# Loading the keys' weights ahead of the tokens in a one-core attention-and-MLP kernel

## The chip, the core and the metric

The kernel runs on one core of a Trainium2 chip. A core has five engines that run side by side, each through its own list of instructions: TensorE (PE, matrix products; its weight loads are shown as PEld), VectorE (DVE), ScalarE (ACT), GpSimd (POOL) and SyncE (SP). In this kernel SP only issues DMA transfers. An engine takes its instructions strictly in order and waits at one until its inputs are there. The metric is device time in microseconds (us) of one execution, as the median of several runs.

## The reference

The input `x` has 2048 tokens of 512 features, in bf16. It is normalised once (`xn`, a layer norm without gain), and two branches read it; their sum is added to `x`.

```python
def _A_ref(x, wqkv, w_phi, wo):        # 32 heads of 16
    q, k, v = split(x @ wqkv)
    pq = einsum("bhsd,hdf->bhsf", q, w_phi)
    pk = einsum("bhsd,hdf->bhsf", k, w_phi)
    phi_q = concat([softmax(pq), softmax(-pq)])     # over the 16 features of a head
    phi_k = concat([softmax(pk), softmax(-pk)])
    kv  = einsum("bhsf,bhsd->bhfd", phi_k, v)
    z   = einsum("bhsf->bhf", phi_k)
    num = einsum("bhqf,bhfd->bhqd", phi_q, kv)
    den = einsum("bhqf,bhf->bhq", phi_q, z)[..., None] + 1e-6
    return (num / den) @ wo

def _B_ref(x, w1, b1, w2):             # 1792 hidden units
    h = x @ w1 + b1
    return (h * tanh(softplus(h))) @ w2

xn = layernorm(x)
out = x + _A_ref(xn, wqkv, w_phi, wo) + _B_ref(xn, w1, b1, w2)
```

## The kernel before

**Tiles.** The 2048 tokens are 16 tiles of 128, in four groups of four. All of `x` stays in `x_sb`; the normalised and transposed tokens stay in `xnT`, in which the features lie on the partitions.

**Folded weights.** The product of a head's `wqkv` columns with its `w_phi` does not depend on the tokens. So the kernel computes the folded keys' weights first (`wkp`, 512 x 512) and projects tokens with them directly. `Wbd` is a block-diagonal arrangement of `w_phi` (tile `wsrc`). Folding needs the keys' weights transposed (`wT`): the row blocks 2 and 3 of the weights come transposed by a DMA (line 483), and the row blocks 0 and 1 come as they are into `wkp` (line 482) and are transposed by TensorE against an identity, then copied into `wT`.

**Order of the work.** Nothing reorders instructions: `manual_schedule` is set, and the string `STEPS` (line 24) is an order written out by a planning run. The loop at line 648 calls one small function per step, and each function appends its instructions to the engines' lists. The `@` number of a step is the PSUM bank, one of six, that it writes; a letter at the end says which engine does a copy or a root (`a` ScalarE, `v` VectorE, `p` GpSimd). So the order of steps is the order in which each engine meets its own instructions. The loads at the start stand ahead of `STEPS` (lines 477 to 493), and the transfers issued by SP start in the order in which SP issues them.

**The head.** These steps come first, until TensorE can run on without pauses:

| step | what it does | engine | line |
|---|---|---|---|
| warm-up | matmuls on constants (`WARM` of 512 columns, `SHORT` of 128) | PE | 514 |
| `LS i`, `RS i` | mean and variance of token tile i; reciprocal root | DVE; ACT or POOL | 165 and 167; 557 or 171 |
| `AZ i` | normalise tile i | DVE | 176 |
| `TP i`, `TC i` | transpose tile i on TensorE; copy it into `xnT` | PE; DVE or ACT | 569; 588 |
| `TW kt`, `TK kt` | transpose row block kt of the keys' weights; copy into `wT` | PE; ACT | 576; 582 |
| `WB` | build `Wbd` from `wsrc` | DVE | 528 |
| `F0 kt`, `FD kt` | fold row block kt; copy it into `wkp` | PE; ACT or DVE | 151; 160 |
| `LP` | keys' logits of token tiles 0 and 1, eight matmuls, row block by row block | PE | 204 |
| `V t`, `VC t` | values of tile t; copy out | PE; ACT or DVE | 189; 213 |
| `L s i`, `LC s i` | logits of tile i of group s; copy out (groups 0 to 3 are keys, 4 to 7 queries) | PE; ACT or DVE | 189; 247 |
| `PB`, `CB` | transpose the bias `b1`; copy it out | PE; DVE | 537; 629 |
| `AM` | load the activation table for the hidden layer | ACT | 139 |

`LP` is ordered by row block: its first two matmuls need `xnT` of tiles 0 and 1 and row block 0 of the folded weights, its last two need row block 3. `FD kt` writes over `wkp`, in which row blocks 0 and 1 lay as they came.

**The rest.** For each group: statistics and normalisation (`LN`, `AP`; `AP` also issues a transposing DMA into `xnT`), the hidden layer (`H` on PE, `M` on ACT, 56 of each), the softmax features (`E` on DVE, `X` on ACT, sums `S` on DVE, `R` and `N` or `W`), the keys' sums into PSUM (`A`, a matmul of features with values, which needs `N`), the masked sums (`KV`), then for queries `Q`, `G`, `C`, and for each token tile the second layer and output projection into one bank (`O`, `P`), the residual and the store (`Y`). The last tile is split in two parts (`OH`, `PH`, `YH`). `DX` and `DW` load further tokens and weights, and `WT` loads and transposes the queries' weights, whose fold is `F`, `FC`.

Of the kernel before, what the change touches and what calls it, by code (L numbers as in the profile page):

```python
# [27 lines left out]
H 10 @0; M 8; H 11 @2; H 12 @1; LN 1; M 9; E 0 0; AP 1 0; AP 1 1; H 13 @4; L 1 0 @3; DX 3; L 1 3 @5;  # L30
DW 2; E 0 1; X 0 1; LN 2; LC 1 0 v; LC 1 3 v; WL 1; LN 3; AP 2 0; AP 2 1; X 0 0; V 6 @3; M 10; M 11;
M 12; H 14 @5; S 0 0; WL 2; LC 1 2 a; VC 6 a; M 13; AP 3 0; H 15 @0; H 16 @2; H 17 @1; LC 1 1 a; AP
3 1; WT; H 18 @3; H 19 @4; M 14; M 15; M 16; M 17; H 20 @5; M 18; M 19; H 21 @0; H 22 @2; H 23 @1; H
24 @3; M 20; M 21; H 25 @4; H 26 @5; M 22; M 23; H 27 @0; M 24; M 25; M 26; M 27; H 28 @2; M 28; H
29 @1; M 29; E 1 0; E 1 1; S 0 1; L 2 1 @3; L 2 0 @4; LC 2 0 v; L 2 2 @5; LC 2 1 v; L 2 3 @0; F 0
@2; R 0 0 a; L 3 2 @1; R 0 1 a; LC 2 2 v; LC 2 3 a; FC 0 a; X 1 0; F 1 @4; F 2 @3; FC 2 a; N 0 0; L
3 0 @5; V 9 @0; LC 3 0 a; V 3 @2; VC 3 a; LC 3 2 v; A 0 0; VC 9 a; V 7 @1; F 3 @3; V 2 @5; VC 7 a; V
8 @2; L 3 3 @0; FC 3 a; X 1 1; VC 2 a; FC 1 v; E 2 0; L 4 0 @4; DW 3; LC 3 3 a; E 2 1; V 4 @1; N 0
1; VC 8 v; X 2 0; S 1 1; LC 4 0 a; S 1 0; L 4 3 @3; VC 4 a; L 4 2 @5; V 11 @0; A 0 1; LC 4 2 a; V 5
@2; VC 11 a; R 1 1 a; S 2 0; L 4 1 @4; LC 4 1 a; L 3 1 @1; VC 5 a; LC 3 1 a; H 30 @5; H 31 @0; LC 4  # L40
3 v; R 1 0 a; M 30; H 32 @4; M 31; M 32; H 33 @2; M 33; N 1 1; H 34 @1; H 35 @3; H 36 @5; M 34; H 37
@0; M 35; H 38 @4; E 3 0; H 39 @2; H 40 @1; M 36; N 1 0; M 37; M 38; M 39; H 41 @3; H 42 @5; H 43
@0; M 40; A 1 0; M 41; E 3 1; M 42; M 43; A 1 1; X 2 1; V 12 @4; VC 12 a; L 5 0 @2; V 10 @1; V 15
@3; VC 15 a; V 13 @5; V 14 @0; E 4 0; E 4 1; LC 5 0 a; VC 13 v; VC 10 a; L 5 2 @4; X 3 1; X 3 0; L 6
3 @3; VC 14 a; L 5 3 @2; O 0 @5; LC 5 2 a; S 2 1; S 3 1; S 3 0; R 3 1 a; R 2 1 a; N 2 1; R 2 0 a; L
6 0 @1; R 3 0 a; N 3 0; L 5 1 @0; LC 5 1 a; N 3 1; O 1 @4; L 6 1 @0; LC 6 0 a; LC 6 3 a; L 6 2 @1; H
44 @3; X 4 0; N 2 0; S 4 0; LC 6 2 a; LC 6 1 v; LC 5 3 a; A 2 0; A 2 1; A 3 0; A 3 1; H 45 @1; X 4
1; M 44; W 4 0 v; H 46 @2; H 47 @0; M 45; M 46; S 4 1; M 47; KV; H 48 @3; M 48; H 49 @1; H 50 @2; M
49; H 51 @0; H 52 @3; M 50; M 51; Q 0 0; H 53 @1; G 0 0; H 54 @2; M 52; Q 0 1; H 55 @0; W 4 1 v; L 7
3 @3; M 53; M 54; E 5 0; G 0 1; L 7 0 @1; E 5 1; Q 1 0; C 0 a; O 2 @2; G 1 0; LC 7 0 a; X 5 0; Q 1  # L50
1; O 3 @1; G 1 1; E 6 0; S 5 0; P 0; P 1; C 1 a; LC 7 3 a; W 5 0 v; L 7 2 @3; M 55; Y 0; O 4 @0; O 5
@5; P 2; LC 7 2 a; Y 1; X 5 1; Q 2 0; G 2 0; L 7 1 @4; E 6 1; LC 7 1 a; P 3; S 5 1; Y 2; W 5 1 v; X
6 0; Q 2 1; G 2 1; O 6 @3; O 7 @2; E 7 0; C 2 a; S 6 0; Y 3; W 6 0 a; E 7 1; Q 3 0; O 8 @4; P 4; Y
4; G 3 0; X 6 1; Q 3 1; G 3 1; X 7 0; S 6 1; C 3 a; O 9 @1; P 5; X 7 1; W 6 1 v; Q 4 0; G 4 0; O 10
@0; Y 5; Q 4 1; G 4 1; S 7 0; C 4 a; O 11 @5; W 7 0 v; Q 5 0; G 5 0; P 6; P 7; Q 5 1; G 5 1; Y 6; O
12 @3; S 7 1; C 5 a; Q 6 0; W 7 1 a; P 8; P 9; G 6 0; Q 6 1; Y 7; Y 8; Y 9; G 6 1; O 13 @2; Q 7 0; C
6 v; G 7 0; P 10; P 11; Y 10; Q 7 1; O 14 @4; G 7 1; P 12; C 7 a; Y 11; Y 12; P 13; OH 0 @1; P 14;
PH 0; OH 1 @0; PH 1; Y 13; Y 14; YH 0; YH 1
"""


# [1 line left out]
def kernel(  # L63
# [410 lines left out]

    part = (slice(0, 384), slice(384, 512))

    for t in range(2):
        nc.sync.dma_start(x_sb[:, t, :], x_v[:, t, :])  # L478
# [3 lines left out]
    nc.sync.dma_start(wkp[:, 0:2, :], wqkv_v[:, 0:2, D : 2 * D])
    nc.sync.dma_start_transpose(
        out=wT_of[0][:, :, 2 * P : 4 * P], in_=A_wqkv[2 * P : 4 * P, D : 2 * D]
    )
    nc.scalar.dma_start(b1b[:], b1_v[:, :])
    with nc.allow_non_contiguous_dma(reason="tiny w_phi load"):
        nc.scalar.dma_start(wsrc[:], wphi_v)
    nc.sync.dma_start(x_sb[:, 2:4, :], x_v[:, 2:4, :])
# [23 lines left out]
    def dummy(n):  # L513
        nc.tensor.matmul(
            warm[:, 0:n], lhsT=nc.const_aps.tensor(1.0, [P, P], BF16),
            rhs=nc.const_aps.tensor(1.0, [P, n], BF16), start=True, stop=True,
        )
# [163 lines left out]
```

## Time and profile before

| | |
|---|---|
| median of 3 runs | 173.78 us (173.75 to 174.08) |
| the profiled execution, its own time | 173.71 us |
| its span | 172.0 us |
| TensorE busy | 168.0 us, 98% |
| VectorE busy | 143.9 us, 84% |
| ScalarE busy | 123.8 us, 72% |
| share of TensorE in the chain that ended last | 95% |

The span runs from the first to the last instruction of the trace; some 1.7 us of the execution lie around it. Times in the trace count from the start of the span. A row of the timeline gives the start, the length, the engine, the line, the operation with its output and input, how many of them were merged into the row, and, in brackets, how long the engine had been idle before it and what released it. SPq and ACTq are the issuing of DMA transfers on those engines. A view by stages gives for each stretch the busy time of each engine with its instruction count, the granted clock of TensorE, the share of the 16 DMA engines and what they moved.

### The profile page before, as it was taken

The page shows a single profiled execution, that of the slowest core. Times are in us where ns is not written, and L with a number is a line of the kernel's source. Part 1 is how long each engine was busy: PE and PEld are TensorE (multiplying, and loading weights), DVE is VectorE, ACT ScalarE, POOL GpSimd, SP SyncE. Part 2 cuts the span into 40 slices and gives each one's busy share as a digit, 9 for nine tenths or more (in the row PEclk, how much of TensorE's full clock was granted, in tenths as well). Part 3 has the DMA queues.
Part 4 walks back from the last instruction along what each step waited for, and adds up shares of the span by engine and source line. Part 5 has one row for each costly group of instructions (what it writes and reads, how often), then busy time and mean ns, then how long its engine had stood idle before and what let it go on. Part 6 is the DMA issues. An engine that isn't in the chain of part 4 may idle for free.

```text
span 172.0 us, 2735 instructions
## 1 busy us (share of the span) xinstructions
PE 168.0 (98%) x1047; PEld 82.6 (48%) x1047; DVE 143.9 (84%) x223; ACT 123.8 (72%) x199; POOL 7.8 (5%) x23
## 2 busy tenths in 40 slices
...
GB/s 124 303 370 248 54 255 347 99 162 228 21 0 0 0 4 0 0 0 0 4 0 0 36 113 99 61 9 150 90 97 116 153 52 197 146 134 216 110 131 61
DMA packets 44185, 18.02 MB, mean 105 GB/s; under 512 B 35980, under 2 KB 44172, under 8 KB 44172
## 3 DMA queue, kind: packets, MB, share of 16 engines
...
## 4 chain that ended last, share of the span: by engine, by line
PE 95%; DMA 2%; SPq 0%; ACT 0%; issue 0%; DVE 0%
PE po L457 28%; PE ph L223 28%; PE pl L189 14%; PE po L464 8%; PE pv L189 8%; PE pnd L412 2%; PE pkv L381 2%; DMA wkp<-in_A_wqkv_dram 2%; PE pl L204 1%; PE pfold L151 1%; PE pwide L189 1%; SPq L478 0%; PE ptr L569 0%; PE ptw L576 0%; ACT wT L582 0%
## 5 line engine op out<-in xcount | busy, mean ns | idle before, releaser
L457 PE MATMUL po<-w_sb,acts 128*128 128x512 bf16 (+2 forms) x238 | 50.8, 366 | 0.0
L223 PE MATMUL ph<-xnT,w_sb 128*128 128x512 bf16 x224 | 49.8, 379 | 0.0
L234 ACT ACTIVATE acts<-ph,b1f 128x512 bf16<-128x512 f32 x56 | 36.3, 701 | 4.2 <-PE ph L223 4.0
L300 DVE TENSOR_REDUCE s<-e 128x128 f32<-128x2048 bf16 x16 | 36.1, 2276 | 0.5 <-ACT e L283 0.5
L223 PEld LDWEIGHTS <-w_sb 128*128 128x128 bf16 x224 | 21.7, 98 | 25.7
L457 PEld LDWEIGHTS <-acts 128*128 128x128 bf16 x238 | 22.1, 98 | 23.6
L283 ACT ACTIVATE e<-e 128x2048 bf16<-128x2048 bf16 x16 | 30.5, 1919 | 0.0
L189 PEld LDWEIGHTS <-xnT 128*128 128x128 bf16 x184 | 17.5, 98 | 19.6
L471 DVE TENSOR_TENSOR x_sb<-po,x_sb 128x512 bf16<-128x512 f32 (+2 forms) x17 | 11.0, 656 | 8.4 <-PE po L464 8.4
L464 PE MATMUL po<-wqk,xnT 128*128 128x512 bf16 (+2 forms) x68 | 15.6, 366 | 0.0
L189 PE MATMUL pv<-wv,xnT 128*128 128x512 bf16 x64 | 15.6, 379 | 0.0
L189 PE MATMUL pl<-wqk,xnT 128*128 128x512 bf16 x64 | 15.4, 379 | 0.0
L427 ACT COPY ds<-pnd 128x32 f32<-128x32 f32 x16 | 2.9, 182 | 16.5 <-PE pnd L412 16.5
L247 ACT CAST p_sb<-pl 128x512 bf16<-128x512 f32 x21 | 12.2, 594 | 3.6 <-PE pl L189 3.4
L139 ACT ACT_TABLE_LOAD x10 | 12.8, 1283 | 0.2
L258 DVE TENSOR_TENSOR m<-m 128x512 bf16<-128x512 bf16 (+1 forms) x32 | 11.5, 359 | 1.1
L189 PE MATMUL pl<-wkp,xnT 128*128 128x512 bf16 x48 | 11.7, 379 | 0.0
L267 DVE TENSOR_TENSOR e<-p_sb,m 128x2048 bf16<-128x2048 bf16 x8 | 9.8, 1226 | 1.8 <-PE pkv L381 1.5
L258 DVE TENSOR_TENSOR m<-p_sb 128x1024 bf16<-128x1024 bf16 x16 | 10.9, 681 | 0.0
L165 DVE BATCH_NORM_STATS2 stats<-x_sb 128x6 f32<-128x512 bf16 x16 | 10.1, 677 | 0.9 <-DMA x_sb<-in_A_x_dram 0.9
L267 DVE TENSOR_TENSOR e<-m,p_sb 128x2048 bf16<-128x2048 bf16 x8 | 9.8, 1225 | 0.3
L334 DVE TENSOR_TENSOR e<-e,r 128x2048 bf16<-128x2048 bf16 x8 | 9.6, 1216 | 0.5 <-ACT r L309 0.5
...
## 6 DMA issues: line engine op xcount, KB each, us to landing
...
out_dram<-x_sb SPq DMA_DIRECT2D x15, 128.0 KB, 1.8
...
x_sb<-in_A_x_dram SPq DMA_DIRECT2D x2, 128.0 KB, 2.1
wkp<-in_A_wqkv_dram SPq DMA_DIRECT2D x1, 256.0 KB, 3.6
x_sb<-in_A_x_dram SPq DMA_DIRECT2D x1, 256.0 KB, 3.6
```

What stands on the lines that cost most here:

```text
L139: nc.scalar.preload_act_table_set(name)
L189: nc.tensor.matmul(pp, lhsT=xnT[:, t, kt, :], rhs=w[:, kt, :], start=(kt == 0), stop=(kt == KT - 1),)
L223: nc.tensor.matmul(ph_of[u][:], lhsT=w1_sb[:, kt, f * P : (f + 1) * P], rhs=xnT[:, g * TPG : (g + 1) * TPG, kt, :], start=(kt == 0), stop= ...
L234: nc.scalar.activation(acts[:, f, g * 512 : (g + 1) * 512], ph_of.pop(u)[:], ACT.Mish, bias=b1f[:, f : f + 1])
L247: copy(p_of[s][:, i, :], pl_of.pop((s, i)))
L258: nc.vector.tensor_tensor(out=m[:], in0=src[:, :, 0:half], in1=src[:, :, half : 2 * half], op=op)
L267: nc.vector.tensor_tensor(out=e_of[s][:].rearrange("p t j l c -> p (t j) l c")[:, :, pl, :].rearrange("p t (c e o) -> p t c e o", e=8, o=2 ...
L283: nc.scalar.activation(v, v, ACT.Exp)
L300: nc.vector.reduce_sum(t[:], pair(s, k).rearrange("p t j l (c e) -> p (t j l c) e", e=16), axis=AX.X)
L457: nc.tensor.matmul(po_of[t, c.stop][:, c], lhsT=acts[:, f, t * P : (t + 1) * P], rhs=w2_sb[:, f, c], start=(f == 0), stop=False,)
L464: nc.tensor.matmul(po_of[t, c.stop][:, c], lhsT=oT_of[t // 2][:, t % 2 * 4 + j, :], rhs=wo_sb[:, j, c], start=False, stop=(j == 3),)
L471: nc.vector.tensor_tensor(out=y, in0=po_of.pop((t, c.stop))[:, c], in1=y, op=ALU.add)
```

## The change

It touches the head in four ways, and the whole `STEPS` string was planned anew with it.

1. SP's loads are put in another order. Before: token tiles 0 and 1 (two transfers of 128 KB), the natural half of the keys' weights (256 KB), their transposed half, token tiles 2 and 3 (256 KB), then `wv`. After: the natural half of the keys' weights, token tiles 0, 1, 2 to 3, the transposed half, then `wv`. From `wv` on the order is the same.
2. On ACT's queue the load of `w_phi` comes first. The bias load, which was ahead of it, now stands behind the load of ScalarE's first activation table.
3. The warm-up matmuls ahead of the steps are six of 512 columns and three of 128, where nine and three stood. Three more of 512 columns (`AW`, which was a 128-column one that no step used) come behind `TW 1`.
4. The steps of the head are laid out anew. On TensorE: `TW 0`, `TW 1`, three `AW`, `F0 0`, `F0 1`, `TP 0`, `TP 1`, `PB`, `F0 2`, `F0 3`, `LP`, `V 1`, `TP 2`, `V 0`, `TP 3`, `L 0 2`, `L 0 3`, `H 0`. Before: `PB`, `TW 0`, `TW 1`, `TP 0`, `TP 1`, `F0 0` to `F0 3`, `LP`, `V 1`, `TP 2`, `V 0`, `TP 3`, `L 0 2`, `H 0`, `L 0 3`, `H 1`. On VectorE `WB` now stands ahead of `AZ 0` and `AZ 1` instead of behind them. All four `FD` are on ScalarE; `FD 1` was on VectorE. `RS 2` is on GpSimd instead of ScalarE. `TC 3` is on ScalarE instead of VectorE. `AM` is gone, so that the table is loaded by the first `M`.

Behind the head the same steps stand in a somewhat different order: `DW 2` (the second layer's weights) behind `WT`, some copies on the other engine, and in the last tiles `OH 0` ahead of `P 12`.

```diff
-WARM, SHORT = 9, 3
+WARM, SHORT = 6, 3
 STEPS = """
-KM; LS 0; RS 0 p; LS 1; RS 1 a; DX 2; PB @0; AZ 0; AZ 1; TW 0 @1; TW 1 @2; TP 0 @3; TP 1 @4; TK 0 a;
-TK 1 a; WB; F0 0 @5; FD 0 a; F0 1 @1; TC 0 v; F0 2 @2; F0 3 @3; FD 2 a; TC 1 v; FD 1 v; FD 3 a; LP i
-@4,5; LS 2; LS 3; RS 2 a; LC 0 0 a; V 1 @1; RS 3 p; AZ 2; TP 2 @2; TC 2 a; VC 1 a; AM; V 0 @3; LC 0
-1 v; AZ 3; CB; TP 3 @4; TC 3 v; L 0 2 @5; LC 0 2 a; H 0 @0; M 0; L 0 3 @2; LC 0 3 a; H 1 @1; M 1; H
...
+TW 0 @0; KM; DX 2; TW 1 @1; AW; AW; AW; TK 0 a; LS 0; LS 1; TK 1 a; WB; RS 0 p; F0 0 @2; F0 1 @3; RS
+1 a; FD 0 a; AZ 0; AZ 1; TP 0 @4; TC 0 v; TP 1 @5; PB @0; TC 1 v; F0 2 @1; FD 1 a; F0 3 @2; FD 2 a;
+FD 3 a; LP i @4,3; V 1 @5; LS 2; RS 2 p; LS 3; AZ 2; TP 2 @1; V 0 @2; CB; RS 3 p; AZ 3; LC 0 0 a; LC
+0 1 v; TP 3 @4; TC 2 a; TC 3 a; VC 0 a; L 0 2 @0; LN 1; L 0 3 @1; H 0 @3; LC 0 2 a; H 1 @4; LC 0 3
...
-    for t in range(2):
-        nc.sync.dma_start(x_sb[:, t, :], x_v[:, t, :])
     wT_of = {0: lnp.tile([P, 4, 512], BF16, name="wT", tag="xn")}
     nc.sync.dma_start(wkp[:, 0:2, :], wqkv_v[:, 0:2, D : 2 * D])
+    for t in (slice(0, 1), slice(1, 2), slice(2, 4)):
+        nc.sync.dma_start(x_sb[:, t, :], x_v[:, t, :])
     nc.sync.dma_start_transpose(
         out=wT_of[0][:, :, 2 * P : 4 * P], in_=A_wqkv[2 * P : 4 * P, D : 2 * D]
     )
-    nc.scalar.dma_start(b1b[:], b1_v[:, :])
     with nc.allow_non_contiguous_dma(reason="tiny w_phi load"):
         nc.scalar.dma_start(wsrc[:], wphi_v)
-    nc.sync.dma_start(x_sb[:, 2:4, :], x_v[:, 2:4, :])
     nc.sync.dma_start(wv[:], wqkv_v[:, :, 2 * D : 3 * D])
...
     nc.scalar.preload_act_table_set(tables[0])
+    nc.scalar.dma_start(b1b[:], b1_v[:, :])
     make_identity(nc, ident[:])
...
-        "KM": masks, "AW": lambda: dummy(P), "WB": weights_by_block, "PB": bias,
-        "AM": lambda: table("mish"), "CB": lambda: nc.vector.tensor_copy(b1f[:], pf_of.pop("b")[:, 0:FT]),
+        "KM": masks, "AW": lambda: dummy(512), "WB": weights_by_block, "PB": bias,
+        "CB": lambda: nc.vector.tensor_copy(b1f[:], pf_of.pop("b")[:, 0:FT]),
```

More of the change, by code (lines that the diff above doesn't have):

```diff
@@ L14 @@
 AX = mybir.AxisListType
-WARM, SHORT = 9, 3
+WARM, SHORT = 6, 3
 STEPS = """
-KM; LS 0; RS 0 p; LS 1; RS 1 a; DX 2; PB @0; AZ 0; AZ 1; TW 0 @1; TW 1 @2; TP 0 @3; TP 1 @4; TK 0 a;
-TK 1 a; WB; F0 0 @5; FD 0 a; F0 1 @1; TC 0 v; F0 2 @2; F0 3 @3; FD 2 a; TC 1 v; FD 1 v; FD 3 a; LP i
-@4,5; LS 2; LS 3; RS 2 a; LC 0 0 a; V 1 @1; RS 3 p; AZ 2; TP 2 @2; TC 2 a; VC 1 a; AM; V 0 @3; LC 0
-1 v; AZ 3; CB; TP 3 @4; TC 3 v; L 0 2 @5; LC 0 2 a; H 0 @0; M 0; L 0 3 @2; LC 0 3 a; H 1 @1; M 1; H
-2 @4; M 2; H 3 @5; H 4 @0; H 5 @2; VC 0 a; H 6 @1; M 3; M 4; M 5; H 7 @4; M 6; M 7; H 8 @3; H 9 @5;
@@ L30 @@
[L30 to L58, printed above, removed]
+TW 0 @0; KM; DX 2; TW 1 @1; AW; AW; AW; TK 0 a; LS 0; LS 1; TK 1 a; WB; RS 0 p; F0 0 @2; F0 1 @3; RS
+1 a; FD 0 a; AZ 0; AZ 1; TP 0 @4; TC 0 v; TP 1 @5; PB @0; TC 1 v; F0 2 @1; FD 1 a; F0 3 @2; FD 2 a;
@@ new lines @@
+FD 3 a; LP i @4,3; V 1 @5; LS 2; RS 2 p; LS 3; AZ 2; TP 2 @1; V 0 @2; CB; RS 3 p; AZ 3; LC 0 0 a; LC
+0 1 v; TP 3 @4; TC 2 a; TC 3 a; VC 0 a; L 0 2 @0; LN 1; L 0 3 @1; H 0 @3; LC 0 2 a; H 1 @4; LC 0 3
+a; E 0 0; H 2 @2; M 0; VC 1 a; H 3 @0; AP 1 0; H 4 @1; M 1; M 2; M 3; M 4; H 5 @3; M 5; H 6 @5; M 6;
+H 7 @4; H 8 @2; H 9 @0; M 7; M 8; H 10 @1; H 11 @3; AP 1 1; DX 3; M 9; L 1 0 @5; E 0 1; LN 2; X 0 1;
+X 0 0; WL 1; L 1 3 @4; M 10; LC 1 0 v; M 11; LC 1 3 v; LC 1 1 a; WL 2; LN 3; AP 2 0; AP 2 1; LC 1 2
@@ new lines @@
+v; AP 3 0; AP 3 1; H 12 @2; H 13 @0; H 14 @5; M 12; H 15 @4; H 16 @1; S 0 1; M 13; M 14; S 0 0; H 17
+@3; WT; H 18 @2; H 19 @0; H 20 @5; M 15; M 16; M 17; M 18; H 21 @4; H 22 @1; M 19; DW 2; H 23 @3; H
+24 @2; M 20; M 21; M 22; H 25 @0; M 23; M 24; H 26 @5; M 25; H 27 @4; E 1 0; M 26; M 27; H 28 @1; H
+29 @3; E 1 1; M 28; M 29; L 2 0 @2; F 0 @0; F 1 @5; R 0 0 a; LC 2 0 a; L 2 1 @4; FC 0 a; L 2 2 @1;
+LC 2 2 v; FC 1 v; L 2 3 @3; LC 2 1 a; L 3 0 @2; LC 2 3 a; F 2 @0; N 0 0; V 9 @1; X 1 1; V 2 @4; FC 2
```

22 lines of the change are left out of this document (added).

## The prediction

> **What bounds the kernel now.** First the page: the span, the busy shares and the chain of work that ended last.
>
> ```profile
> span 172.0 us, 2735 instructions
> ...
> PE 168.0 (98%) x1047; PEld 82.6 (48%) x1047; DVE 143.9 (84%) x223; ACT 123.8 (72%) x199; POOL 7.8 (5%) x23
> ...
> PE 95%; DMA 2%; SPq 0%; ACT 0%; issue 0%; DVE 0%
> ```
>
> TensorE is busy for nearly the whole span and makes up almost the whole chain. The view by stages then tells where its idle time lies (start and end, length, PE, PEld, DVE, ACT, POOL, each with its instruction count, granted clock, DMA share, GB/s):
>
> ```profile
> 14.40:169.30 154.90, 154.90 (x966) 75.95 (x964) 134.17 (x200) 114.69 (x183) 4.38 (x6) 1.00 0.41 89
> ```
>
> From 14.40 us until the last products TensorE never pauses: 154.90 us busy of 154.90. Behind that stage no VectorE or ScalarE work sets the end. What can be won or lost lies in the head, or in a pause that the new order brings into the stage that now has none. So the timeline of the head:
>
> ```profile
> 0.79 0.88 SPq L478 DMA_DIRECT2D x_sb<-in_A_x_dram  x2
> ...
> 0.83 4.00 PE L514 MATMUL warm<-const-bfloat16-1.0 128*128 128x512 bf16 x12 [0.83 <-PEq L665]
> ...
> 1.47 0.41 ACTq L488 DMA_DIRECT2D wsrc<-in_A_w_phi_dram  x1
> ...
> 1.72 0.43 SPq L482 DMA_DIRECT2D wkp<-in_A_wqkv_dram  x1
> ...
> 2.19 1.32 SPq L483 DMA_TRANSPOSE wT<-in_A_wqkv_dram  x1
> ...
> 2.95 0.69 DVE L165 BATCH_NORM_STATS2 stats<-x_sb 128x6 f32<-128x512 bf16 x1 [0.35 <-DMA x_sb<-in_A_x_dram]
> ...
> 3.56 0.57 SPq L489 DMA_DIRECT2D x_sb<-in_A_x_dram  x1
> ...
> 4.47 0.18 DVE L167 BATCH_NORM_AGGREGATE mv<-stats 128x2 f32<-128x6 f32 x1
> ...
> 4.87 0.85 DVE L176 TENSOR_SCALAR xn<-x_sb,mv,rstd 128x512 bf16<-128x512 bf16 x2 [0.22 <-POOL rstd L172]
> ...
> 5.36 0.62 PE L576 MATMUL ptw<-ident,wkp 128*128 128x128 bf16 x8 [0.42 <-DMA wkp<-in_A_wqkv_dram]
> 5.64 0.42 DVE L528 TENSOR_TENSOR Wbd<-block,wsrc 128x512 bf16<-128x512 bf16 x1
> ...
> 5.79 1.07 ACT L582 CAST wT<-ptw 128x512 bf16<-128x512 f32 x2 [0.51 <-PE ptw L576]
> ...
> 6.24 0.76 DVE L588 COPY xnT<-ptr 128x512 bf16<-128x512 bf16 x2 [0.18 <-PE ptr L569]
> ...
> 6.43 1.33 PE L151 MATMUL pfold<-Wbd,wT 128*128 128x128 bf16 x16
> 6.87 1.78 ACT L160 CAST wkp<-pfold 128x512 bf16<-128x512 f32 x3
> ...
> 7.55 0.37 PEld L204 LDWEIGHTS <-xnT 128*128 128x128 bf16 x3
> 7.60 1.95 PE L204 MATMUL pl<-wkp,xnT 128*128 128x512 bf16 x8
> ...
> 9.39 1.03 PE L189 MATMUL pv<-wv,xnT 128*128 128x512 bf16 x4
> ```
>
> TensorE's rows overlap at their ends, as the last result of a batch comes out some 0.17 us after the next batch has begun. From `V 1` (9.39) on TensorE runs without a break, and everything behind it is the same amount of work in both kernels. So I reduce the question to one number: **when does `V 1` start?** Before it is 9.39; the profiled span is 172.0, so 162.6 us follow it.
>
> Read backwards, 9.39 is the eight matmuls of `LP`, which start at 7.60, as soon as the first fold is back in SBUF (ACT, 6.87 plus 0.59). That fold (6.43) waited for the first copy into `wT` (5.79), this for `TW 0` (5.36), and `TW 0` for the natural half of the keys' weights, issued at 1.72. The token side was ahead of it: both `TC` copies were over at 7.00. The transfers' times from issue to landing:
>
> ```profile
> x_sb<-in_A_x_dram SPq DMA_DIRECT2D x2, 128.0 KB, 2.1
> wkp<-in_A_wqkv_dram SPq DMA_DIRECT2D x1, 256.0 KB, 3.6
> ...
> wsrc<-in_A_w_phi_dram ACTq DMA_DIRECT2D x1, 16.0 KB, 4.0
> wT<-in_A_wqkv_dram SPq DMA_TRANSPOSE x1, 4.2
> ```
>
> So `x` tile 0 landed at 0.79 + 2.1 = 2.89 (VectorE starts on it at 2.95), tile 1 near 3.3, the weights' natural half at 1.72 + 3.6 = 5.32, `w_phi` at 1.47 + 4.0 = 5.47, the transposed half at 2.19 + 4.2 = 6.39. The fold of row blocks 2 and 3 could use that at 6.9, so the transposed half was not late.
>
> **The change part by part.** *Loads on SP.* The issue times add up from the rows, with 0.05 between two of them: the weights' natural half at 0.79 (0.43 long), tile 0 at 1.27, tile 1 at 1.7, tiles 2 and 3 near 2.2 (0.57), the transposed half at 0.79 + 0.43 + 0.88 + 0.57 + 0.14 = 2.81, `wv` near 4.2 as before. What is pulled ahead is the weights' natural half; what pays is `x` tile 0, which now has 256 KB in front of it where it had nothing.
>
> *When does tile 0 land (X)?* No row shows it, so it is bounded by these stretches:
>
> ```profile
> 1.60:2.80 1.20, 1.20 (x4) 0.44 (x3) 0.22 (x1) 0.89 (x1) 0.92 (x6) 1.00 0.74 213
> 2.20:2.80 0.60, 0.60 (x3) 0.16 (x2) 0.22 (x1) 0.60 (x1) 0.39 (x5) 1.00 0.99 324
> 2.80:4.80 2.00, 2.00 (x9) 0.79 (x7) 1.64 (x4) 0.45 (x2) 0.77 (x2) 1.00 0.99 197
> ```
>
> The first one (213 GB/s in 1.2 us) is the two token tiles, 256 KB: all out by 2.8, and the second landed at 1.24 + 2.1 = 3.3, so a transfer lands about 0.5 behind its bytes. Lower end: the second 128 KB transfer landed 2.1 after its issue with 128 KB ahead; another 128 KB ahead at 324 GB/s adds 0.4, so X = 1.27 + 2.5 = 3.75, or 3.3 if the larger queue costs nothing. Upper end: the weights take 3.6 again (landing at 4.39) and tile 0 comes behind them at 197 GB/s, 0.65 more: X = 5.05. The third stretch is the weights' own: 197 GB/s, little more than half of the second, with `w_phi`'s small pieces (issued at 1.47) in flight. `w_phi` is now issued at the same moment as the weights, so this is the nearest row: 384 KB from 1.6 at 197 GB/s are out at 3.55, and X = **4.05**. I take that, and keep 3.3 and 5.05 for the range. The Trainium skill, "DMA: Bandwidth & Descriptors", section "Issuing engines are not separate DMA queues", says that transfers started by different engines run on the same 16 DMA engines and interleave. By that rule `w_phi` on ACT's queue does slow the loads on SP's, and X is 4.05; were the queues independent, it would be 3.75. The slow third stretch agrees with the rule, though a transposing transfer is issued in it too.
>
> *The chain from tile 0 to `V 1`.* Tile 0's landing to the end of `LS 1`: 2.89 to 4.65, 1.76 (tile 1 comes in time, 0.85 of `LS 0` later). Then `WB`, which the new order puts ahead of `AZ`: 0.42, with handover 0.45. `w_phi`, issued 0.7 earlier, lands near 4.8, before that. `AZ 0` and `AZ 1`: 0.85. Then a transposition and its copy, as with tile 3:
>
> ```profile
> 10.74 0.41 DVE L176 TENSOR_SCALAR xn<-x_sb,mv,rstd 128x512 bf16<-128x512 bf16 x1 [0.18 <-POOL rstd L172]
> ...
> 11.21 0.35 PEld L569 LDWEIGHTS <-xn 128*128 128x128 bf16 x4 [0.20 <-DVE xn L176]
> 11.34 0.39 PE L569 MATMUL ptr<-ident,xn 128*128 128x128 bf16 x4
> ...
> 11.77 0.42 DVE L588 COPY xnT<-ptr 128x512 bf16<-128x512 bf16 x1 [0.53 <-PE ptr L569]
> ```
>
> The product's weights load 0.06 after `AZ` ends (11.15 to 11.21); from there to the product 0.05 where PE is free (7.55 to 7.60), and 0.43 to the copy: 0.54, then 0.42 for `TC 1`. The second matmul of `LP` needs it: 0.07, and seven matmuls of 0.216 (1.73 for eight in 7.60 to 9.33) are 1.51. Sum 1.76 + 0.45 + 0.85 + 0.54 + 0.42 + 0.07 + 1.51 = 5.60. `V 1` starts at X + 5.6, so the break-even is X = 3.79.
>
> *The other branches of that join.* The folds: `WB` done at X + 2.2; fold 0 to its copy 0.44 plus 0.07; four copies, now all on ACT, 0.59 each: X + 5.1; the last two matmuls of `LP` 0.5: X + 5.6, a tie. The transposed half, by its 4.2, lands at 7.0; fold, two copies and two matmuls (0.5 + 1.18 + 0.5) give 9.2, below 9.65. It could be faster, now that `w_phi` is past by then:
>
> ```profile
> xnT<-xn SPq DMA_TRANSPOSE x6, 3.4
> ```
>
> By this 3.4 it lands at 6.2 (8.4 at `V 1`). `TW 0` starts at 3.4 to 4.4 instead of 5.36, a gain of 1 to 2 us that goes nowhere: its fold waits for `WB`, near 6.2, about where fold 0 stood (6.43).
>
> *Edits at nothing.* Three warm-ups fewer ahead and three `AW` behind `TW 1` (at most 1.3 us) fill time in which PE waits for `WB`; their cover is gone if X is below 2. The bias transfer behind the table load lands long before `PB`, which stands behind `TP 1`. `RS 2` on POOL is followed by `AZ 2`, which is needed by `TP 2`, four matmuls of `V 1` later; I take 0, and 0.1 as an estimate of the other end. `TC 3` on ACT, `L 0 3` ahead of `H 0`, and no `AM`: the table load falls on ACT while four banks of `H` are free; 0. Bytes ahead of `wv` and the MLP weights are the same, so they land as before.
>
> *The sum.* 4.05 + 5.6 = 9.65 against 9.39: +0.26 on the profiled 172.0 span and 173.71 us, so 173.97 there; the median lies 0.07 above the profiled execution: **174.0**. That is +0.15%, within what a measurement can tell (0.2%, 0.35 us).
>
> **The rivals.** *Faster.* Tile 0 lands 2.1 after its issue as tile 1 did, X = 3.37, and the transposed half at 6.2 to 6.8: `V 1` at 8.97, -0.4, 173.35 us. For it: the rate of 324 GB/s in the second stretch. Against: the third. It decides below X = 3.44.
>
> *Slower, by `w_phi` in the way.* X above 4.14 is worth over 0.35 us; at the upper end, 5.05, `V 1` starts at 10.65, +1.26, 175.0. For it: the weights took 3.6 with `w_phi` in flight. Against: part of that time a transposing transfer was in flight too.
>
> *Slower, by the clock.* The warm-ups run at half rate:
>
> ```profile
> 3.77 0.15 PEld L514 LDWEIGHTS <-const-bfloat16-1.0 128*128 128x128 bf16 x1 [0.28 <-issue]
> ...
> 4.20 0.45 PEld L514 LDWEIGHTS <-const-bfloat16-1.0 128*128 128x128 bf16 x3 [0.28 <-issue]
> ```
>
> 0.43 per 512 columns, where `LP` takes 0.216; the transpositions of 5.36 are at full rate. The granted clock column says 1.00 throughout, so the pace is the evidence. Now 0.83 + 6 x 0.43 + 3 x 0.11 = 3.7 ends them. If the weights land at 4.4, PE pauses for 0.7 and full rate may come late: fold 0 and `TP 1` at half rate are +0.4 (174.2), seven matmuls of `LP` too +1.5 more (175.7). The Trainium skill, "TensorE: Matmul & The Clock Gate", Part 1, says that about 3.4 us of sustained activity lift the half rate, in a window that runs freely. By it six warm-ups (2.9 us) are too few by themselves, and the forecast needs `TW` and `AW` to follow at once. The trace agrees so far as nine warm-ups (4.00 us) sufficed.
>
> *Slower, by a new wait behind the head.* VectorE is the nearest engine. The tightest place that I find by counting steps is `A 1 0`, which waits for `N 1 0`:
>
> ```profile
> 68.60 1.22 DVE L334 TENSOR_TENSOR e<-e,r 128x2048 bf16<-128x2048 bf16 x1
> 69.74 0.68 DVE L258 TENSOR_TENSOR m<-p_sb 128x1024 bf16<-128x1024 bf16 x1
> ...
> 71.57 1.23 DVE L267 TENSOR_TENSOR e<-m,p_sb 128x2048 bf16<-128x2048 bf16 x1
> ...
> 74.77 1.18 PE L381 MATMUL pkv<-vext,e 128*128 128x65 bf16 x32
> ```
>
> Before, `N 1 0` ends at 69.8 and `A 1 0` starts at 74.8. The new order puts one more `E` half ahead of it (69.74 to 72.80, 3.0): 2 us of cover are left. A wait of 0.4 to 1 us elsewhere would make 174.4 to 175.
>
> **How the numbers follow.** Forecast, X from 3.44 to 4.14, 0.38; faster 0.17; `w_phi` 0.28; clock 0.10; a new wait 0.07. Slower is the last three, 0.45. The likeliest single case gives 174.0 (its own range 173.4 to 174.1). The range for 8 in 10 takes the faster case and all of `w_phi`'s to its upper end: 173.3 to 175.0.
>
> **What would show it.** Right: tile 0's `LS 0` starts near 4.1, `WB` ends near 6.3, `TW 0` starts before 4.4 and fold 0 follows only on `WB`, `V 1` starts near 9.65, PE is full from 14.4 on. Wrong: `LS 0` before 3.5 (faster) or after 4.2; matmuls of `LP` 0.43 apart; `LP` waiting for fold 2 because the transposed half landed after 7.5; a PE wait behind 14.4.

## The result and the profile after

The changed kernel takes 181.14 us (median of 6 runs, 180.54 to 182.08) against 173.76 us of the kernel before in the same session (173.39 to 174.08): a ratio of 1.0431, with a 95% interval of 1.0412 to 1.0451. The forecast was 174.0 us, and its range ended at 175.0. The change costs 7.4 us, and most of that lies far behind the head that the change is about.

The page of the changed kernel, with the lines that answer to those quoted of before (span, busy shares, TensorE's busy share and granted clock in 40 slices, the chain that ended last):

```profile
span 179.4 us, 2719 instructions
...
PE 169.7 (95%) x1031; PEld 83.6 (47%) x1047; DVE 143.2 (80%) x222; ACT 125.2 (70%) x199; POOL 8.6 (5%) x25
...
PEclk9999997599999999999999999999999999999999
...
PE 89%; ACT 5%; DMA 2%; DVE 1%; issue 1%; SPq 0%
```

Two things are new. ScalarE has 5% of the chain, where it had nothing, and in two slices (from 26.9 and from 31.4 us on) the granted clock is down to 0.7 and 0.5. The view of the waits names the place:

```profile
PE pwide L190 <- ACT p_sb L248: 4.5, 1, 4.5
```

Behind the head TensorE waited once, for 4.5 us. The timeline around it (start, length, engine, line, operation; in brackets the idle time before it and what ended it):

```profile
24.73 3.71 ACT L284 ACTIVATE e<-e 128x2048 bf16<-128x2048 bf16 x2
...
25.13 1.03 PE L190 MATMUL pwide<-wkp,xnT 128*128 128x512 bf16 x4
...
25.99 1.03 PE L190 MATMUL pl<-wkp,xnT 128*128 128x512 bf16 x4
...
28.46 1.28 ACT L140 ACT_TABLE_LOAD   x1
29.75 1.27 ACT L235 ACTIVATE acts<-ph,b1f 128x512 bf16<-128x512 f32 x2
...
30.91 0.58 ACT L248 CAST p_sb<-pwide 128x512 bf16<-128x512 f32 x1
...
31.54 1.86 PE L190 MATMUL pwide<-wkp,xnT 128*128 128x512 bf16 x4 [4.52 <-ACT p_sb L248]
...
32.35 0.15 PEld L190 LDWEIGHTS <-xnT 128*128 128x128 bf16 x1 [0.28 <-issue]
32.78 0.15 PEld L224 LDWEIGHTS <-w_sb 128*128 128x128 bf16 x1 [0.28 <-issue]
```

`WL 1` and `WL 2`, steps that the prediction does not mention, project token tiles 1 and 2 of group 1 into the two halves of one PSUM tile, `pwide` (line 620 of the changed kernel; each half is as wide as one of the six banks). (The row at 25.99 is `L 1 3`.) The row at 25.13 is `WL 1`, that at 31.54 is `WL 2`. The copy at 30.91 is `LC 1 1`, which empties the first half. In the new order it is issued ahead of `WL 2`, and `WL 2`, which writes the other half, waits for it. `LC 1 1` stands on ScalarE behind both `X` of group 0 (3.71 us), a table load (1.28) and `M 10` and `M 11` (1.27); in that time TensorE has, behind `WL 1`, only `L 1 3` left. In the kernel before, these rows stand so:

```profile
24.13 3.71 ACT L283 ACTIVATE e<-e 128x2048 bf16<-128x2048 bf16 x2
...
27.11 1.03 PE L189 MATMUL pwide<-wkp,xnT 128*128 128x512 bf16 x4
...
29.70 1.03 PE L189 MATMUL pwide<-wkp,xnT 128*128 128x512 bf16 x4
...
32.39 0.62 ACT L247 CAST p_sb<-pwide 128x512 bf16<-128x512 f32 x1
```

There `WL 2` (29.70) is issued ahead of `LC 1 1` (32.39), and nothing waits. The description of the change names neither this exchange nor that `V 6` and `H 14`, which stood between `WL 1` and `WL 2`, stand elsewhere now.

The pause has an after-effect. Windows over it (start and end, length, PE, PEld, DVE, ACT, POOL with their counts, granted clock, DMA share, GB/s):

```profile
27.00:28.00 1.00, 0.02 (x1) 0.00 (x0) 0.94 (x2) 1.00 (x1) 0.70 (x1) 1.00 0.00 0
...
29.00:29.20 0.20, 0.00 (x0) 0.00 (x0) 0.20 (x1) 0.20 (x1) 0.00 (x0) 0.84 0.00 0
29.20:29.40 0.20, 0.00 (x0) 0.00 (x0) 0.20 (x1) 0.20 (x1) 0.00 (x0) 0.50 0.00 0
...
35.80:36.00 0.20, 0.20 (x2) 0.11 (x1) 0.20 (x1) 0.04 (x1) 0.00 (x0) 0.59 0.00 0
36.00:36.20 0.20, 0.20 (x2) 0.10 (x1) 0.20 (x1) 0.00 (x0) 0.00 (x0) 1.00 0.52 104
```

TensorE stops at 27.02, and the clock falls to half inside the slice from 29.00: a mean of 0.84 there puts the fall at 29.14, 2.1 us into the pause. In the slice from 35.80 a mean of 0.59 puts the rise at 35.96. From 31.54 to 35.96 TensorE thus works at half rate (weight loads 0.43 apart at 32.35 and 32.78, as in the warm-ups): 4.42 us in which 2.21 us of work at full rate get done.

The head, in the same form:

```profile
3.90 1.03 PE L576 MATMUL ptw<-ident,wkp 128*128 128x128 bf16 x8
...
4.55 0.69 DVE L166 BATCH_NORM_STATS2 stats<-x_sb 128x6 f32<-128x512 bf16 x1 [1.95 <-DMA x_sb<-in_A_x_dram]
...
6.17 0.39 DVE L528 TENSOR_TENSOR Wbd<-block,wsrc 128x512 bf16<-128x512 bf16 x1
...
6.61 0.61 PE L152 MATMUL pfold<-Wbd,wT 128*128 128x128 bf16 x8 [0.81 <-DVE Wbd L528]
...
8.28 1.89 PE L205 MATMUL pl<-wkp,xnT 128*128 128x512 bf16 x7
...
10.01 0.81 PE L190 MATMUL pv<-wv,xnT 128*128 128x512 bf16 x3
```

Tile 0 landed at 4.5, and `V 1` started at 10.01 instead of 9.39. The 7.4 us of span are then accounted for: 0.62 in the head, 4.52 of pause, 2.21 of half rate, together 7.35.

### The profile page after: what moved, and what is told of

The parts are those of the page before. It is cut to its first block, busy times and chain, and to the rows that moved or that the text cites. A ratio compares the mean times of both kernels' runs of the same rounds, so it can differ in the third digit from the quotient of the medians.

```text
span 179.4 us, 2719 instructions
## 1 busy us (share of the span) xinstructions
PE 169.7 (95%) x1031; PEld 83.6 (47%) x1047; DVE 143.2 (80%) x222; ACT 125.2 (70%) x199; POOL 8.6 (5%) x25
## 4 chain that ended last, share of the span: by engine, by line
PE 89%; ACT 5%; DMA 2%; DVE 1%; issue 1%; SPq 0%
PE ph L224 27%; PE po L458 27%; PE pl L190 12%; PE pv L190 8%; PE po L465 8%; PE pnd L413 2%; PE pkv L382 2%; ACT e L284 2%; DMA x_sb<-in_A_x_dram 2%; ACT L140 1%; PE pfold L152 1%; ACT acts L235 1%; PE pwide L190 1%; PE pl L205 1%; DVE stats L166 1%
## 5 line engine op out<-in xcount | busy, mean ns | idle before, releaser
L224 PE MATMUL ph<-xnT,w_sb 128*128 128x512 bf16 x224 | 51.2, 386 | 0.1
L235 ACT ACTIVATE acts<-ph,b1f 128x512 bf16<-128x512 f32 x56 | 37.0, 692 | 9.6 <-PE ph L224 9.2
L465 PE MATMUL po<-wqk,xnT 128*128 128x512 bf16 (+2 forms) x66 | 15.0, 366 | 0.1
L248 DVE CAST p_sb<-pl 128x512 bf16<-128x512 f32 x8 | 5.5, 683 | 8.0 <-PE pl L190 7.8
```

The lines of the kernel that those rows point to most:

```text
L224: nc.tensor.matmul(ph_of[u][:], lhsT=w1_sb[:, kt, f * P : (f + 1) * P], rhs=xnT[:, g * TPG : (g + 1) * TPG, kt, :], start=(kt == 0), stop= ...
L235: nc.scalar.activation(acts[:, f, g * 512 : (g + 1) * 512], ph_of.pop(u)[:], ACT.Mish, bias=b1f[:, f : f + 1])
L248: copy(p_of[s][:, i, :], pl_of.pop((s, i)))
L465: nc.tensor.matmul(po_of[t, c.stop][:, c], lhsT=oT_of[t // 2][:, t % 2 * 4 + j, :], rhs=wo_sb[:, j, c], start=False, stop=(j == 3),)
```

## The experiments

**The pause: order, cause and price.** The first theory is the reading above: the new wait of `WL 2` costs some 6.8 us, and the head is worth the rest. Its rival: the pause is a symptom, and something else in the new order (ScalarE being late, or a transfer) costs the time. Five runs test it.

*The two steps exchanged*, in the changed kernel:

```diff
-LC 1 3 v; LC 1 1 a; WL 2; LN 3;
+LC 1 3 v; WL 2; LC 1 1 a; LN 3;
```

> The changed kernel with one step moved: WL 2 stands just ahead of the copy LC 1 1 instead of behind it. Theory (WL 2 writes the other half of the PSUM tile that LC 1 1 reads, and so waits for that copy, which stands behind two exponentials on ScalarE; the clock then falls because of the pause): the pause of 4.52 us at 27.0 and the half-rate stretch of 4.54 us behind it (2.27 us lost) go, 181.14 - 6.79 = 174.35, granted clock 1.00 throughout; what is left, +0.6, is the head. Rival (ScalarE is late as a whole, and TensorE would wait for it at the next bank anyway): the pause comes back at H 16, which needs the bank that M 10 frees, and the time is 177 or more.

Measured: 174.67 us, 1.0056 of the kernel before (1.0034 to 1.0078), span 173.3, granted clock 1.00 in the mean. TensorE's timeline:

```profile
25.86 1.03 PE L190 MATMUL pwide<-wkp,xnT 128*128 128x512 bf16 x4
26.73 1.03 PE L190 MATMUL pl<-wkp,xnT 128*128 128x512 bf16 x4
27.59 1.03 PE L190 MATMUL pwide<-wkp,xnT 128*128 128x512 bf16 x4
```

No pause, no fall of the clock: 6.5 of the 7.4 us go with one step's place. What is left belongs to the head, where `V 1` waited 0.49 for `wv` in this profile and started at 10.73.

*The wait brought into the kernel before*, by the opposite exchange:

```diff
-S 0 0; WL 2; LC 1 2 a; ... H 17 @1; LC 1 1 a; AP
+S 0 0; LC 1 1 a; WL 2; LC 1 2 a; ... H 17 @1; AP
```

> The kernel before with the opposite edit: LC 1 1, which stood behind WL 2, is put just ahead of it. Theory: WL 2 now waits for that copy, which ScalarE reaches after M 12, near 31.7, instead of starting at 29.7 to 29.9; TensorE pauses about 1.9 us, short of the 2.5 us after which the clock fell in the changed kernel; 173.76 + 1.9 = 175.7, clock near 1.00. Rival (the two halves of the tile are independent, and the pause in the changed kernel had another cause): no change, 173.8.

Measured: 175.71 us, 1.0117 (1.0092 to 1.0141).

```profile
31.60 1.02 PE L189 MATMUL pwide<-wkp,xnT 128*128 128x512 bf16 x4 [1.66 <-ACT p_sb L247]
```

The same wait, 1.66 us here because more TensorE work stands between. The four matmuls behind it take 1.02, as at full rate: this pause was too short for the clock to fall. (The windows above put the fall 2.1 us into the changed kernel's pause; the 2.5 of the expectation is too long.)

*The copy on VectorE* in the changed kernel, the order left:

```diff
-LC 1 1 a; WL 2;
+LC 1 1 v; WL 2;
```

> The changed kernel with the order of steps kept, and only the copy LC 1 1 given to VectorE, which reaches it near 27.7, behind LC 1 3. Theory: WL 2 starts near 28.4, the pause shrinks from 4.5 to 1.4 us, the clock does not fall: 181.14 - 3.1 - 2.27 = 175.8. Rival (ScalarE is late as a whole): 177 or more, with the pause moved to H 16.

Measured: 176.22 us, 1.014 (1.0111 to 1.017).

```profile
11.27 1.04 PE L190 MATMUL pv<-wv,xnT 128*128 128x512 bf16 x4 [0.98 <-DMA wv<-in_A_wqkv_dram]
...
29.69 1.02 PE L190 MATMUL pwide<-wkp,xnT 128*128 128x512 bf16 x4 [1.40 <-DVE p_sb L248]
```

The wait follows the copy to the other engine and its queue, and again the clock stays up. (The head cost more in this execution, 11.27 for `V 1`, because `wv` came late; that is taken up below.)

*The pause filled* with 20 matmuls on constants in a free bank, ahead of `WL 2`:

```diff
+    def keep_busy(b):
+        fill = bank(b, "fill")
+        for _ in range(20):
+            nc.tensor.matmul(fill[:], lhsT=<ones 128x128>, rhs=<ones 128x512>, start=True, stop=True)
...
-LC 1 1 a; WL 2;
+LC 1 1 a; AK @2; WL 2;
```

> The changed kernel with 20 matmuls of 512 columns on constants ahead of WL 2, in a free bank: 4.3 us of work that fills the pause and lengthens nothing. Theory: WL 2 still waits until about 31.5, but the clock stays at 1.00, so only the half-rate loss goes: 181.14 - 2.27 = 178.9. If the clock falls for another reason than the pause, 181.1 again.

Measured: 179.56 us, 1.0338 (1.0315 to 1.0361).

```profile
26.90 4.54 PE L525 MATMUL fill<-const-bfloat16-1.0 128*128 128x512 bf16 x20
31.59 1.02 PE L190 MATMUL pwide<-wkp,xnT 128*128 128x512 bf16 x4 [0.15 <-ACT p_sb L248]
...
163.37 0.43 PE L413 MATMUL pnd<-kvm,qT 128*128 128x68 bf16 x8 [0.50 <-DMA qT<-e]
```

`WL 2` starts as late as before, but at full rate, and 1.6 us are saved. The forecast was the whole 2.2; 0.5 of the difference of about 0.7 shows as a wait for a transposed query tile at 163, which the profile of the changed kernel without the fill does not have. So pause and half rate are two costs, and the second falls away when TensorE is kept busy.

*A PSUM bank of its own for `WL 2`*, the order left (from `H 12` on the banks are renamed among themselves, so that bank 2 is free there):

```diff
         if i == 1:
             wide_of[0] = ps2.tile([P, 2, 512], FP32, name="pwide", tag="kv")
-        pl_of[1, i] = project(wkp, TPG + i, wide_of[0][:, i - 1, :])
+            pl_of[1, i] = project(wkp, TPG + i, wide_of[0][:, 0, :])
+        else:
+            pl_of[1, i] = project(wkp, TPG + i, bank(b, "pl")[:])
...
-LC 1 1 a; WL 2;
+LC 1 1 a; WL 2 @2;
```

> The changed kernel with WL 2 in a PSUM bank of its own instead of the second half of the tile that LC 1 1 reads; LC 1 1 stays ahead of WL 2. (From H 12 on the six banks are renamed among themselves, so that the one used is free.) Theory: the wait comes from the shared tile, so it goes, and with it the fall of the clock: about 174.7 us, as with the two steps exchanged, up to 175.2 if H 17 waits for the copy that empties the new bank. Rival: the order of LC 1 1 and WL 2 makes the wait by itself, or WL 2 waits for something else at the same time: 181 us as before this edit.

Measured: 174.93 us, 1.0051 (1.002 to 1.0081).

```profile
26.23 1.89 PE L190 MATMUL pl<-wkp,xnT 128*128 128x512 bf16 x8
27.96 5.42 PE L224 MATMUL ph<-xnT,w_sb 128*128 128x512 bf16 x23
...
31.16 0.58 ACT L248 CAST p_sb<-pwide 128x512 bf16<-128x512 f32 x1
```

`L 1 3` and `WL 2` run back to back at 26.23, more than 4 us ahead of `LC 1 1` at 31.16, though this still precedes `WL 2` in the order. So it is the shared tile that makes the wait: a write of one half waits for the read of the other. The run gives `WL 2` another tile and with it other waits; whether the chip itself would have needed this wait is not shown. The Trainium skill, "Perfetto Trace Analysis", section "Matmuls", advises to rotate independent groups of matmuls through different PSUM banks, so that the copies of one overlap the matmuls of the next. The trace agrees only with an addition: the halves of `pwide` are each as wide as one of the six banks, and it took two tiles to free them of each other.

**The head.** With the pause gone, the changed kernel still loses about 0.5%. In ten profiles, that of the kernel before and nine of the runs below and above, the span less the start of `V 1` is 162.6 us within 0.05, for starts from 9.39 to 11.80. (The run with a bank of its own has 162.9.) So the prediction's reduction to one number holds, once a pause is excluded, and the question is what `V 1` waits for. The runs change one load or one group of loads at a time; "changed, exchanged" is the first run above.

*SP's loads in the old order*, with `w_phi` first on ACT's queue, on the changed, exchanged kernel:

```diff
-    nc.sync.dma_start(wkp[:, 0:2, :], wqkv_v[:, 0:2, D : 2 * D])
-    for t in (slice(0, 1), slice(1, 2), slice(2, 4)):
+    for t in (slice(0, 1), slice(1, 2)):
         nc.sync.dma_start(x_sb[:, t, :], x_v[:, t, :])
+    nc.sync.dma_start(wkp[:, 0:2, :], wqkv_v[:, 0:2, D : 2 * D])
     nc.sync.dma_start_transpose(
         out=wT_of[0][:, :, 2 * P : 4 * P], in_=A_wqkv[2 * P : 4 * P, D : 2 * D]
     )
+    nc.sync.dma_start(x_sb[:, 2:4, :], x_v[:, 2:4, :])
```

> The changed kernel with WL 2 ahead of LC 1 1, and SP's loads in the order of before (token tiles 0 and 1, then the weights' natural half, the transposed half, tiles 2 and 3); w_phi still first on ACT's queue. Theory (the head is late because tile 0 lands at 4.5 behind 256 KB, and V 1 starts 5.5 after it): tile 0 lands near 3.0, WB ends near 5.2, the weights land at 4.4 to 4.9, V 1 starts at 8.9 to 9.2 against 10.0 to 10.7 and 9.39 before: 173.2 to 173.5, slightly below before (173.6). Rival (the new order of steps is what costs): V 1 stays at 10 or later, 174.7.

Measured: 175.23 us, 1.0075 (1.005 to 1.0099), against expectation.

```profile
3.16 0.69 DVE L166 BATCH_NORM_STATS2 stats<-x_sb 128x6 f32<-128x512 bf16 x1 [0.57 <-DMA x_sb<-in_A_x_dram]
...
5.26 1.03 PE L577 MATMUL ptw<-ident,wkp 128*128 128x128 bf16 x8 [1.40 <-DMA wkp<-in_A_wqkv_dram]
...
7.37 1.06 PE L152 MATMUL pfold<-Wbd,wT 128*128 128x128 bf16 x8
7.44 0.42 DVE L177 TENSOR_SCALAR xn<-x_sb,mv,rstd 128x512 bf16<-128x512 bf16 x1 [1.94 <-ACT rstd L559]
...
11.80 0.38 PE L190 MATMUL pv<-wv,xnT 128*128 128x512 bf16 x1
```

Tile 0 is there 1.4 us sooner, but the new steps do not fit the old loads. Six warm-ups end 1.4 us ahead of the weights; after that pause TensorE is still at half rate, which the warm-ups had not left, through `TW` and the folds (eight matmuls of a fold take 1.06, not 0.61). And the root of tile 1 stands on ScalarE behind `TK 0` and `TK 1`, which wait for the weights, so `AZ 1` waits 1.94. The clock rival, absent from the changed kernel, is real here; how much of the delay it makes, and how much the root, is not separated. (The profile is of the slowest of the twelve executions, 176.09 us, so 11.80 is above the usual start.)

*The bias first again on ACT's queue* (`w_phi` behind it), on the changed, exchanged kernel:

```diff
+    nc.scalar.dma_start(b1b[:], b1_v[:, :])
     nc.scalar.dma_start(wsrc[:], wphi_v)
...
     nc.scalar.preload_act_table_set(tables[0])
-    nc.scalar.dma_start(b1b[:], b1_v[:, :])
```

> The changed kernel with WL 2 ahead of LC 1 1, SP's loads in the new order, and the bias load ahead of w_phi on ACT's queue as before. Theory that w_phi's small pieces slow the loads beside them: tile 0 lands near 3.9 instead of 4.55, V 1 starts near 9.5, 174.0. Rival (the 256 KB ahead cost what they cost, whatever w_phi does): tile 0 at 4.5, 174.7.

Measured: 174.21 us, 1.0035 (1.001 to 1.006). *No `w_phi` transfer at all*, on the same kernel:

```diff
-        nc.scalar.dma_start(wsrc[:], wphi_v)
+    nc.gpsimd.memset(wsrc[:], 0.01)
```

> The changed kernel with WL 2 ahead of LC 1 1 and without the load of w_phi: its tile is filled with a constant by GpSimd, so the features are not the reference's; all other work is the same. Theory that w_phi's pieces slow the loads: tile 0 lands at 3.75 instead of 4.55, V 1 starts near 9.3, 173.8. Rival (the 256 KB alone): tile 0 at 4.5, 174.7.

Measured: 174.22 us, 1.0015 (0.999 to 1.004). *`w_phi` first in the kernel before*, with `PB` behind `TP 1`:

```diff
-KM; LS 0; RS 0 p; LS 1; RS 1 a; DX 2; PB @0; AZ 0; AZ 1; TW 0 @1; TW 1 @2; TP 0 @3; TP 1 @4; TK 0 a;
+KM; LS 0; RS 0 p; LS 1; RS 1 a; DX 2; AZ 0; AZ 1; TW 0 @1; TW 1 @2; TP 0 @3; TP 1 @4; PB @0; TK 0 a;
...
-    nc.scalar.dma_start(b1b[:], b1_v[:, :])
     nc.scalar.dma_start(wsrc[:], wphi_v)
...
     nc.scalar.preload_act_table_set(tables[0])
+    nc.scalar.dma_start(b1b[:], b1_v[:, :])
```

> The kernel before with only w_phi put first on ACT's queue and the bias load behind the table load (PB goes behind TP 1, so that it does not hold TensorE up for the bias). Theory that w_phi held up the weights' natural half: this lands at 4.4 to 4.6 instead of 5.3, TW 0 starts as much earlier, V 1 starts near 9.0 (then the token copies bind), 173.2. Rival (no influence, or tile 0 is slowed as much instead): 173.6 or more.

Measured: 174.23 us, 1.0023 (1.0003 to 1.0043). The start of `LS 0` on the timeline of the run with the bias first:

```profile
4.27 0.69 DVE L166 BATCH_NORM_STATS2 stats<-x_sb 128x6 f32<-128x512 bf16 x1 [1.67 <-DMA x_sb<-in_A_x_dram]
```

The same without `w_phi`:

```profile
4.02 0.69 DVE L166 BATCH_NORM_STATS2 stats<-x_sb 128x6 f32<-128x512 bf16 x1 [1.35 <-DMA x_sb<-in_A_x_dram]
```

And with `w_phi` first in the kernel before, with its start of `V 1`:

```profile
3.23 0.69 DVE L165 BATCH_NORM_STATS2 stats<-x_sb 128x6 f32<-128x512 bf16 x1 [0.64 <-DMA x_sb<-in_A_x_dram]
...
9.99 1.04 PE L189 MATMUL pv<-wv,xnT 128*128 128x512 bf16 x4 [0.35 <-DMA wv<-in_A_wqkv_dram]
```

With 2.95 before, 4.55 in the changed kernel and 4.49 to 4.73 in its variants with the same loads, this gives the parts of tile 0's delay of 1.6: about 1.1 for 256 KB of weights ahead (4.02 against 2.95), 0.2 more with `w_phi` issued second, 0.5 to 0.7 more with `w_phi` issued first. (These are single profiles, and the same loads differ by up to 0.24, so the 0.2 is uncertain.) `w_phi` first costs 0.3 even in the old order of loads (3.23 against 2.95), and its earlier arrival bought nothing there. The rows also show a new waiter: `V 1` waits for `wv`.

*The weights' natural half first, alone*, in the kernel before:

```diff
-    for t in range(2):
-        nc.sync.dma_start(x_sb[:, t, :], x_v[:, t, :])
     nc.sync.dma_start(wkp[:, 0:2, :], wqkv_v[:, 0:2, D : 2 * D])
+    for t in range(2):
+        nc.sync.dma_start(x_sb[:, t, :], x_v[:, t, :])
```

> The kernel before with the other part alone: the natural half is loaded ahead of tiles 0 and 1 (w_phi stays behind the bias, steps as before). Theory: tile 0 lands about 1.2 us later, at 4.1 to 4.2, and V 1 starts 5.4 later, at 9.6: 174.0 to 174.2 us. Rival (the earlier transposition of the weights pays): TW 0 starts at 4 instead of 5.4 and V 1 before 9.2: below 173.7 us.

Measured: 174.98 us, 1.008 (1.0054 to 1.0107), slower than expected.

```profile
4.24 0.69 DVE L165 BATCH_NORM_STATS2 stats<-x_sb 128x6 f32<-128x512 bf16 x1 [1.64 <-DMA x_sb<-in_A_x_dram]
...
8.57 1.89 PE L204 MATMUL pl<-wkp,xnT 128*128 128x512 bf16 x8
...
10.30 1.03 PE L189 MATMUL pv<-wv,xnT 128*128 128x512 bf16 x4
```

Tile 0 comes as late as forecast, but `V 1` starts 6.1 behind it, not 5.4. The place where this is lost is ahead of `LP`: it starts 4.33 behind `LS 0`, against 3.73 in the changed kernel (8.28 and 4.55), as the old order has `WB` behind `AZ` and the folds behind `TP`. From `LP` to `V 1` both take 1.73, so `wv` held nothing up here. So putting the weights first is a loss by itself, and by these rows the new steps of the head win part of it back (`V 1` at 10.01); the times themselves, 174.98 and 174.67 us, have intervals that overlap.

*The transposed half's transfer behind tiles 2 and 3, alone*, in the kernel before:

```diff
-    nc.sync.dma_start_transpose(
-        out=wT_of[0][:, :, 2 * P : 4 * P], in_=A_wqkv[2 * P : 4 * P, D : 2 * D]
-    )
...
     nc.sync.dma_start(x_sb[:, 2:4, :], x_v[:, 2:4, :])
+    nc.sync.dma_start_transpose(
+        out=wT_of[0][:, :, 2 * P : 4 * P], in_=A_wqkv[2 * P : 4 * P, D : 2 * D]
+    )
```

> The kernel before with one part of the change alone: the transposed half's transfer stands behind tiles 2 and 3 on SP's queue. Theory: without the transposing transfer beside it the natural half lands at 4.9 instead of 5.3, the transposed half at about 7.0, still ahead of the fold that needs it; V 1 starts near 9.2 and the time is about 173.5 us. Rival: the natural half is slowed by something else (w_phi, the tiles) and lands at 5.3 as before, or the transposed half is late for the third fold: 173.7 us or more.

Measured: 173.93 us, 0.9998 (0.9984 to 1.0013): no difference.

```profile
0.82 4.32 PE L514 MATMUL warm<-const-bfloat16-1.0 128*128 128x512 bf16 x12 [0.82 <-PEq L665]
...
5.20 0.98 PE L576 MATMUL ptw<-ident,wkp 128*128 128x128 bf16 x8
...
9.44 1.03 PE L189 MATMUL pv<-wv,xnT 128*128 128x512 bf16 x4
```

`TW 0` no longer waits for the weights and starts 0.16 sooner. But it runs at half rate, 0.98 for what took 0.62 from 5.36 on, and `V 1` starts at 9.44 against 9.39. Before, the same twelve warm-ups took 4.00 and not 4.32: full rate came sooner in that execution.

*Nine warm-ups in front again*, and *`WB` ahead of `LS 0`*, each on the changed, exchanged kernel:

```diff
-WARM, SHORT = 6, 3
+WARM, SHORT = 9, 3
```

> The changed kernel with WL 2 ahead of LC 1 1 and with all nine warm-ups in front again (three AW stay). TW 0 moves from 3.9 to about 4.7; the folds wait for the mask of w_phi at 6.2 to 6.6 in any case. Theory: the split of the warm-ups is worth nothing here: 174.6 us as without this edit, within 0.3. Rival (the head hangs on TW): 175.2 us or more.

```diff
-TK 0 a; LS 0; LS 1; TK 1 a; WB; RS 0 p;
+TK 0 a; WB; LS 0; LS 1; TK 1 a; RS 0 p;
```

> The changed kernel with WL 2 ahead of LC 1 1 and with WB ahead of LS 0 on VectorE, which takes 0.42 us out of the chain from tile 0 to V 1. Theory: w_phi lands at 4.1, before tile 0 at 4.5, so WB costs tile 0 nothing: V 1 at about 9.6 if the values' weights have landed by then, 174.2 us. Rival: V 1 waits for the values' weights as it did in the run without this edit, and nothing is won: 174.6 us.

Measured: 174.58 us, 1.0039 (1.0023 to 1.0055), and 174.66 us, 1.0037 (1.002 to 1.0055). Neither edit changes the time. With nine warm-ups `TW` comes later, and with it `TK` and tile 1's root behind it on ScalarE: `LP` starts 4.02 behind `LS 0` (8.51 and 4.49) instead of 3.73. That this costs nothing is owed to `wv`, which landed at 10.2. Of the second run:

```profile
8.23 1.89 PE L205 MATMUL pl<-wkp,xnT 128*128 128x512 bf16 x8
10.34 1.04 PE L190 MATMUL pv<-wv,xnT 128*128 128x512 bf16 x4 [0.22 <-DMA wv<-in_A_wqkv_dram]
```

`LP` starts only 0.05 sooner than in the changed kernel, since GpSimd's root of tile 0 takes up most of the time that `WB` left, and then `V 1` waits for `wv`. With the pause removed, `wv` and tile 0 hold the head between them. `wv` lands 4.6 after its issue before (at 8.8, not awaited), 5.4 in the changed kernel, and 4.8 to 7.1 in the other runs; the higher values come with the weights or `w_phi` ahead, but they differ between kernels with the same loads (5.4 to 7.1), so what sets them stays open.

No version among these beats the kernel before.

## Why the prediction was wrong

**The step that failed** is the rival "a new wait behind the head", and the sentence on which it and the reduction rest: that from `V 1` on everything is the same work, with "VectorE is the nearest engine" and "the tightest place that I find by counting steps is `A 1 0`". I went by VectorE's steps; the wait is on TensorE, for ScalarE, at 27 us. `A 1 0` did not wait at all. I gave it 0.07 and a price of 0.4 to 1 us; it cost 4.52, and 2.21 more by the clock. The rows of before would have given nearly the first figure. `LC 1 1` now stands behind both `X`, a table load and two `M`: 3.71 + 1.28 + 1.27 before its own 0.6, some 6.9 us from the start of `X`, while TensorE has `WL 1` and `L 1 3` to do, 1.7 us, and the rest of a projection begun before. What I did not ask is whether a step that moved past another shares a tile with it.

**The clock** was priced only in the head. There it cost nothing in the changed kernel: `TW` at 3.90 was at half rate (1.03 for eight), the folds at 6.61 at full rate (0.61), and `TW 0` began 0.04 us after the warm-ups had ended (0.82 + 3.04 = 3.86). The fall of the clock after a later pause was in no term.

**X, the landing of tile 0**, was the mis-sized term: 4.05 taken, 4.5 measured. Inside its ends of 3.3 and 5.05, but on the side of the rival "`w_phi` in the way", which was given 0.28. The part without `w_phi` was taken at 3.75 and measured at 4.0; `w_phi`'s share was taken at 0.3 and measured at 0.5 to 0.7. The rule of interleaving quoted from the Trainium skill, "DMA: Bandwidth & Descriptors", points the right way: 16 KB on another engine's queue delayed SP's tiles.

**What held.** The chain from tile 0 to `V 1` was forecast at 5.6 and took 5.5. `WB` ended at 6.56, 2.05 behind tile 0's landing, where 2.2 was forecast. `TW 0` started at 3.90, between 3.4 and 4.4, and its gain went nowhere: the first fold waited 0.81 for `WB`. The warm-ups' split was worth nothing in time (run with nine: 174.58 against 174.67), but partly by luck, as `wv` hid the 0.3 by which `LP` came later with nine. From the start of `V 1` the time follows one for one, wherever TensorE has no pause. So the head came to +0.62 where +0.26 was forecast, and alone would have put the time near 174.4; the exchanged kernel took 174.67, because its `V 1` waited for `wv` too, which I had at "land as before" (4.6 from issue to landing before, 5.4 in the changed kernel).
